# Order of the first loads, a row of identity products at the start, and the order of the last output blocks in a fused attention and two-MLP kernel

## The chip, the cores and the metric

The kernel runs on one core of one Trainium2 chip. The metric is the device time of one execution in microseconds (us); lower is better. The core has five engines that run side by side and meet through semaphores: TensorE (PE in the profile, with its weight loads as PEld), VectorE (DVE), ScalarE (ACT), GpSimd (POOL) and SyncE (SP), which here only issues DMAs. Each engine works through its own instructions in order, so an instruction that waits holds up everything behind it on that engine.

## The reference

Inputs are q, k and v of shape (4, 12, 448, 64), and the weights of two gated MLPs.

```python
scores = q @ k.T / sqrt(64) - log(448)
attn_out = sigmoid(scores) @ v                       # per batch and head
x = attn_out with the heads side by side             # (4, 448, 768)

# MLP 1, then MLP 2 with its own weights
h = act(x @ w_in)                                    # relu, then gelu (tanh form)
u, v = h[..., :512], h[..., 512:]
v_n = (v - mean(v)) / sqrt(var(v) + 1e-6)            # MLP 2 also times g_ln
v_s = einsum('ts,bsd->btd', w_spatial, v_n) + b_spatial[None, :, None]
x = (u * v_s) @ w_out                                # MLP 2 adds its input x
```

The weights w_in and w_out arrive as 8-byte floats, the others as 4-byte ones.

## The kernel before

Most products are made in a fast 4-byte matmul format whose operands are split into a high part (a rounded copy) and a low part (the rest), three products for one. Values times attention is made in plain 4-byte floats.

**Attention** runs over NG = 12 groups of four heads (three groups for each of four batches) in steps s = 4n + r, where n is the group and r a block of 128 keys (the last has 64). Step s issues, in this order: `scores(n, r)` on PE (L357) and the sigmoid of them on ACT (L368); `values` of step s - 2 on PE (L381), which adds up in two PSUM banks for a group; at r = 1 `gather(n - 1)` on DVE (L395), which copies the previous group's sums out of those two banks; and one third of the operands of group n + 1: `turn` (transposes, DVE, r = 0), `high` (copies, DVE and ACT, r = 1), `low` (subtractions, L337, one half on DVE and one on POOL, r = 2). The pool for the value sums has two banks in all, so the first `values` of group n + 1 (step 4n + 6) waits for `gather(n)` (step 4n + 5).

Loads are issued by SP in program order. Before the loop come `load_qk(0)`, `load_qk(1)` (two DMAs each) and `load_v(0)` (eight DMAs). In the loop `load_v(1)` comes at s = 0, `load_qk(n + 2)` at r = 1 and `load_v(n + 2)` at r = 2, so values are two groups ahead.

**Conversion of the weights** is spread over the run by a `Belt`: each `tick(new)` moves every running job by one stage and then starts `new` more. A job `convert` is: load 256 KB (SP, L158); make a 4-byte float from the 8-byte one (DVE L169, L173, L177, with a square on POOL L164 or ACT L168); finish it (DVE L183); cast the high part (ACT L191); subtract for the low part (L193). In attention one piece starts in each of the steps 0 to 7 and then in every second step. A second belt, `spatial`, does the same for the four slices of `w_spatial` with `load_w_sp`: four DMAs; nothing; transpose and two casts on DVE (L226 to L228); subtract and copy on DVE (L230, L231). A slice has one of two buffers. It ticks from s = 42 on, so slice j is transposed at step 44 + j.

**The MLPs** run block by block: for each batch `hv` (L474) makes the half that is normalised, `hu` (L519) the other, `sp` (L538) the product over the sequence, and `wo` (L572) the output product. After each of these comes a `fill`, which ticks the belts. `split_x` (L462 on ACT, L463 on DVE) makes the high and low part of a block's input; for the first block it stands at s = 48, behind the last scores.

**The end.** The last `wo` runs over six output columns blocks m; when one is done DVE adds the input (L582). `store_last` then transposes block c on PE (L609) with the identity, copies it out of PSUM (ACT L616, DVE L614) and stores it (L620, L623), in pairs of blocks. It is called for block m - 2 behind the products of block m.

Of the kernel before, what the change touches and what calls it, by code (L numbers as in the profile page):

```python
# [9 lines left out]
F32 = mybir.dt.float32  # L10
# [15 lines left out]
def tile_sigmoid_attention_two_gated_mlps(  # L26
# [59 lines left out]
    def bank():  # L86
        return later["ps_t"].tile([P, 512], F32, tag="t", name="t")
# [186 lines left out]
    def attention(apool, epool, ps_att, done):  # L274
# [13 lines left out]
        def load_v(n):  # L288


            b, i = divmod(n, G)
            vt = epool.tile([P, 4, 3, D], F32, tag="v", name="vt", bufs=3)
            vr = epool.tile([P, 2, D], F32, tag="vr", name="vr", bufs=3)
            src = v[b, 4 * i:4 * i + 4].rearrange("h (t c) d -> t h c d", c=TC)
            for e in range(4):
                ts = slice(32 * e, 32 * e + 32)
                nc.sync.dma_start(
                    out=vt[ts].rearrange("p h c d -> p h (c d)"),
                    in_=src[:, :, 3 * e:3 * e + 3].rearrange("t h c d -> t h (c d)"),
                )  # L300
                hs = slice(2 * (e // 2), 2 * (e // 2) + 2)
                nc.sync.dma_start(out=vr[ts], in_=src[:, hs, 12 + e % 2])
            vs[n] = vt, vr
# [106 lines left out]
        load_qk(0)  # L410
        load_qk(1)
        load_v(0)
        turn(0)
        high(0)
        low(0)
        for s in range(4 * NG + 2):
# [9 lines left out]
            if n + 1 < NG:  # L426
# [3 lines left out]
                    high(n + 1)  # L430
                elif r == 2:
                    low(n + 1)
            if n + 2 < NG:
                if r == 1:
                    load_qk(n + 2)
                elif r == 2:
                    load_v(n + 2)
            if s == 0:
                load_v(1)
            elif s == 4 * NG - 9:  # L440
                load_vecs(l1)
            belt.tick(1 if s < 8 else s % 2)
            if s >= 4 * NG - 6:
                spatial.tick(1)
        return lambda: gather(NG - 1)

# [1 line left out]
    class Mlp:  # L448
# [111 lines left out]
        def wo(self, b, i, after=None):  # L560
# [8 lines left out]
            for m in range(KD):  # L569
# [7 lines left out]
                for c in done if i == KF - 1 else ():  # L577
                    x = xs[b // 2][:, c, (b % 2) * S:(b % 2 + 1) * S]
                    if L.n == 1:
                        nc.scalar.copy(out=x, in_=self.o[c][:, :S])  # L580
                    else:
                        nc.vector.tensor_tensor(out=x, in0=self.o[c][:, :S], in1=x, op=ALU.add)  # L582
                if after and m > 1:
                    after(m - 2)
            if after:
                after(KD - 2)
                after(KD - 1)

    def store(pool, b, m):

# [13 lines left out]

    def store_last(o, pr, m):

        t = bank()
        for j in range(3, 7):
            nc.tensor.transpose(  # L609
# [2 lines left out]
        dst, src = o[:, :, m * P:(m + 1) * P], t.rearrange("p (j f) -> p j f", j=4)  # L612
        if m == KD - 2:
            nc.vector.tensor_copy(out=dst, in_=src)  # L614
        else:
            nc.scalar.copy(out=dst, in_=src)  # L616
        if m % 2:
            ms = slice((m - 1) * P, (m + 1) * P)
            eng = nc.scalar if m == KD - 1 else nc.sync
            nc.sync.dma_start(  # L620
                out=out[2 * pr + 1, :3 * P, ms].rearrange("(j p) m -> p j m", p=P), in_=o[:, 1:, ms]
            )
            eng.dma_start(out=out[2 * pr + 1, 3 * P:, ms], in_=o[REST:, 0, ms])  # L623

    with tc.manual_schedule():
        make_identity(nc, ident)
# [22 lines left out]
        with tc.tile_pool(name="fpool", bufs=1) as fpool:  # L649
# [9 lines left out]
            for n, (m, b) in enumerate(seq):  # L659
# [3 lines left out]
                def fill(new=0, more=(), waits=False):  # L663
# [8 lines left out]
                    if waits:  # L672
                        chain.tick()

                def split_next(c):
                    if nxt:
                        nxt.split_x(nb, c, c + 2)
# [39 lines left out]
                m.sp(b, 1)  # L717
                fill(0 + refill, waits=True)
                m.wo(b, 0)
                fill(1, w_o(0))  # L720
                split_next(2)
                m.sp(b, 2)
                if refill:
                    spatial.waiting = [load_w_sp(l2, j) for j in range(4)]
                fill(0 + refill, waits=True)
                m.wo(b, 1)
                fill(1, w_o(1))
                split_next(4)
                m.sp(b, 3)
                fill(1, waits=True)  # L730
                m.wo(b, 2)
                fill(0 + refill, w_o(2))
                if refill:
# [44 lines left out]
```

## Time and profile before

| | us |
|---|---|
| median of 3 runs | 597.12 (595.78 to 597.28) |
| the profiled execution, its own time | 597.48 |
| its span, first to last instruction | 595.7 |

| engine | busy us | share of the span |
|---|---|---|
| PE | 571.4 | 96% |
| DVE | 410.0 | 69% |
| ACT | 251.6 | 42% |
| POOL | 98.9 | 17% |

The page gives the busy time of each engine over the span, and what an engine waited for. Since PE is busy nearly all the time, one reads first where it is not: a table of the run in stretches shows that. In each stretch one then looks for the wait that ended last. All times in the rows are counted from the span's start.

### The profile page before, as it was taken

The page shows a single profiled execution, that of the slowest core. Times are in us where ns is not written, and L with a number is a line of the kernel's source. Part 1 is how long each engine was busy: PE and PEld are TensorE (multiplying, and loading weights), DVE is VectorE, ACT ScalarE, POOL GpSimd, SP SyncE. Part 2 cuts the span into 40 slices and gives each one's busy share as a digit, 9 for nine tenths or more (in the row PEclk, how much of TensorE's full clock was granted, in tenths as well). Part 3 has the DMA queues.
Part 4 walks back from the last instruction along what each step waited for, and adds up shares of the span by engine and source line. Part 5 has one row for each costly group of instructions (what it writes and reads, how often), then busy time and mean ns, then how long its engine had stood idle before and what let it go on. Part 6 is the DMA issues. An engine that isn't in the chain of part 4 may idle for free.

```text
span 595.7 us, 9520 instructions
## 1 busy us (share of the span) xinstructions
PE 571.4 (96%) x3568; PEld 456.5 (77%) x3568; DVE 410.0 (69%) x805; ACT 251.6 (42%) x418; POOL 98.9 (17%) x127
## 2 busy tenths in 40 slices
PE   4969999999999999999999999999999999999996
PEld 2535555555469888998888899888989988998995
DVE  4599999999976985894688357669444545544433
ACT  4647877787724434433423345534221313212112
POOL 0445465445221001000200100020010002001000
PEclk9979999999999999999999999999999999999999
DMA  6854446545311212532242224520004100500502
GB/s 185 226 182 136 139 145 196 166 138 119 62 60 35 72 53 72 159 107 62 87 153 80 80 73 114 123 54 18 1 1 77 17 0 12 83 1 0 82 13 92
DMA packets 85405, 51.74 MB, mean 87 GB/s; under 512 B 56112, under 2 KB 75376, under 8 KB 85360
## 3 DMA queue, kind: packets, MB, share of 16 engines
q1 hardware_dynamic: 85280, 51.08, 31.7%
q8 instruction: 28, 0.46, 0.3%
q14 instruction: 17, 0.14, 0.1%
q10 hardware_dynamic: 80, 0.07, 0.0%
HBM read 41.68 MB, written 9.44 MB: 86 GB/s over the span
## 4 chain that ended last, share of the span: by engine, by line
PE 73%; DVE 13%; DMA 4%; issue 3%; ACT 3%; POOL 2%; SPq 1%; DVEq 0%; ACTq 0%
PE t L519 13%; PE t L474 12%; PE sc L572 12%; PE av L381 10%; PE sc L357 10%; PE t L538 10%; PE av L572 6%; DMA w<-in_moe_w_in_dram 2%; DVE f L177 2%; DVE f L173 1%; DMA inq<-in_q_dram 1%; DVE st L483 1%; DVE f L183 1%; POOL st L488 1%; DVE vr L493 1%
## 5 line engine op out<-in xcount | busy, mean ns | idle before, releaser
L368 ACT ACTIVATE a<-sc,small 128x896 f32<-128x896 f32 (+1 forms) x96 | 92.8, 1006 | 32.6 <-PE sc L357 32.3
L357 PEld LDWEIGHTS sc<-ops 32*128 32x128 f32 x1152 | 57.5, 194 | 46.5 <-ACT a L368 25.2
L357 PE MATMUL sc<-ops 32*128 32x448 f32 x1152 | 80.0, 397 | 9.0 <-ACT ops L328 7.5
L519 PE MATMUL t<-xh,uh 128*128 128x448 f32 x192 | 69.9, 364 | 0.9 <-ACT u L523 0.9
L485 POOL TENSOR_SCALAR st<-st 128x1 f32<-128x1 f32 x28 | 10.6, 378 | 356.7 <-DVE st L484 356.7
L381 PE MATMUL av<-a,vt 128*64 128x448 f32 x288 | 64.7, 572 | 5.2 <-DVE x L395 5.0
L519 PE MATMUL t<-xh,ul 128*128 128x448 f32 x192 | 69.5, 362 | 0.0
L519 PE MATMUL t<-xl,uh 128*128 128x448 f32 x192 | 69.3, 361 | 0.0
L474 PE MATMUL t<-vh,xl 128*128 128x512 f32 x168 | 65.7, 391 | 1.3 <-DVE xl L463 1.2
L538 PE MATMUL t<-sh,v 128*128 128x448 f32 x224 | 65.9, 363 | 0.6 <-DVE gt L544 0.6
L474 PE MATMUL t<-vh,xh 128*128 128x512 f32 x168 | 65.6, 390 | 0.0
L474 PE MATMUL t<-vl,xh 128*128 128x512 f32 x168 | 65.4, 389 | 0.0
L551 ACT CAST gh<-u 128x448 fp32r<-128x448 f32 x32 | 18.2, 567 | 103.6 <-DVE u L550 103.6
L483 DVE BATCH_NORM_STATS2 st<-vr 128x6 f32<-128x512 f32 x28 | 19.4, 694 | 53.6 <-ACT vr L480 53.6
L183 DVE SCALAR_TENSOR_TENSOR f<-g,f 128x256 f32<-128x256 f32 x72 | 47.1, 654 | 9.2 <-ACT g L168 3.9
L572 PE MATMUL sc<-gl,oh 128*128 128x448 f32 x128 | 46.7, 365 | 2.1 <-DVE gl L555 2.1
L572 PE MATMUL sc<-gh,oh 128*128 128x448 f32 x128 | 46.5, 363 | 0.0
L572 PE MATMUL sc<-gh,ol 128*128 128x448 f32 x128 | 46.4, 362 | 0.0
L538 PE MATMUL t<-sl,v 128*128 128x448 f32 x128 | 46.3, 362 | 0.0
L538 PEld LDWEIGHTS t<-sh,v 128*128 128x128 f32 x224 | 42.0, 188 | 3.9 <-DVE gt L544 1.2
L381 PEld LDWEIGHTS av<-a,vt 128*64 128x64 f32 x288 | 18.2, 140 | 34.8 <-issue 25.6
L501 ACT CAST v<-vr 128x512 fp32r<-128x512 f32 x24 | 14.9, 621 | 66.0 <-DVE vr L493 66.0
(87 smaller groups left out, 1019.4 us busy)
## 6 DMA issues: line engine op xcount, KB each, us to landing
w<-in_moe_w_in_dram SPq DMA_DIRECT2D x48, 256.0 KB, 3.6
w<-in_moe_w_out_dram SPq DMA_DIRECT2D x24, 256.0 KB, 2.8
ink<-in_k_dram SPq DMA_DIRECT2D x12, 448.0 KB, 4.2
inq<-in_q_dram SPq DMA_DIRECT2D x12, 448.0 KB, 5.1
vt<-in_v_dram SPq DMA_DIRECT2D x48, 96.0 KB, 2.5
out_dram<-y SPq DMA_DIRECT2D x72, 56.0 KB, 1.9
kept<-f SPq DMA_DIRECT2D x30, 128.0 KB, 1.7
w<-kept SPq DMA_DIRECT2D x12, 192.0 KB, 2.6
```

Source lines behind the costliest of these rows:

```text
L177: nc.vector.scalar_tensor_tensor(out=f, in0=high, scalar=-0x40000000, in1=f, op0=ALU.bitwise_and, op1=ALU.bitwise_or)
L183: nc.vector.scalar_tensor_tensor(out=f, in0=g, scalar=TINY * TINY, in1=f, op0=ALU.is_ge, op1=ALU.mult)
L357: nc.tensor.matmul(sc[h // 2][:, h % 2, :S], w[ps, o:o + P], ops[n][ps, y, S * j:S * (j + 1)], start=(t == 0), stop=(t == 5), tile_positio ...
L368: nc.scalar.activation(a[:, 2 * x:2 * x + 2] if r < 3 else a[ps], sc[x][ps, :, :S], AF.Sigmoid, bias=bias_s[ps], scale=scale,)
L381: nc.tensor.matmul(avp[n][x][o * D:(o + 1) * D, :S], vt[:, h, r] if r < 3 else vr[ps, o], a[:, h] if r < 3 else a[ps, o], start=(r == 0), ...
L474: nc.tensor.matmul(ps[:, :FF], a, w[:, c, :], start=(c == 0 and n == 0), stop=(c == KD - 1 and n == 2),)
L483: nc.vector.bn_stats(out=st, in_=vr)
L501: nc.scalar.copy(out=pair[0], in_=vr)
L519: nc.tensor.matmul(ps[:, :S], w, a, start=(c == 0 and n == 0), stop=(c == KD - 1 and n == 2))
L538: nc.tensor.matmul(ps[:, :S], a, w, start=(n == 0), stop=(n == len(todo) - 1))
L551: nc.scalar.copy(out=gh, in_=u)
L572: nc.tensor.matmul(self.o[m][:, :S], w, a, start=(i == 0 and n == 0), stop=(i == KF - 1 and n == 2),)
```

## The change

In words:

- Values are loaded one group ahead instead of two: `load_v(n + 1)` at r = 2, in two buffers instead of three; `load_v(1)` goes from s = 0 to s = 2.
- The first piece of weights is started ahead of the loop, right behind `load_v(0)`; step 0 doesn't tick, so every later piece starts in the step in which it did.
- 18 products of the identity with itself stand ahead of everything else on PE; nothing reads them.
- `load_vecs` and the four `w_spatial` slices start two steps earlier (37 instead of 39, 40 instead of 42).
- In the first MLP block three of the fills start no new piece.
- At the end `store_last` is called three blocks late instead of two; the last block's add is split in two, its copy between ACT and DVE; blocks 4 and 5 are stored one by one; and the short DMA of a pair goes ahead of the long one.

```diff
-            vt = epool.tile([P, 4, 3, D], F32, tag="v", name="vt", bufs=3)
-            vr = epool.tile([P, 2, D], F32, tag="vr", name="vr", bufs=3)
+            vt = epool.tile([P, 4, 3, D], F32, tag="v", name="vt", bufs=2)
+            vr = epool.tile([P, 2, D], F32, tag="vr", name="vr", bufs=2)
...
         load_v(0)
+        belt.tick(1)
+
+        warm = ps_att.tile([P, 2, 512], F32, tag="sc", name="sc")
+        for _ in range(18):
+            nc.tensor.matmul(warm[:, 0, :P], ident, ident, start=True, stop=True)
         turn(0)
...
-            if n + 2 < NG:
-                if r == 1:
-                    load_qk(n + 2)
-                elif r == 2:
-                    load_v(n + 2)
-            if s == 0:
-                load_v(1)
-            elif s == 4 * NG - 9:
+            if r == 1 and n + 2 < NG:
+                load_qk(n + 2)
+            elif r == 2 and n + 1 < NG:
+                load_v(n + 1)
+            if s == 4 * NG - 11:
                 load_vecs(l1)
-            belt.tick(1 if s < 8 else s % 2)
-            if s >= 4 * NG - 6:
+            if s > 0:
+                belt.tick(1 if s < 7 else s % 2)
+            if s >= 4 * NG - 8:
                 spatial.tick(1)
...
-                    else:
-                        nc.vector.tensor_tensor(out=x, in0=self.o[c][:, :S], in1=x, op=ALU.add)
-                if after and m > 1:
-                    after(m - 2)
+                        continue
+                    h = S - 2 * P if after and c == KD - 1 else 0
+                    for ts in ((slice(0, h), slice(h, S)) if h else (slice(0, S),)):
+                        nc.vector.tensor_tensor(
+                            out=x[:, ts], in0=self.o[c][:, ts], in1=x[:, ts], op=ALU.add
+                        )
+                if after and m > 2:
+                    after(m - 3)
             if after:
-                after(KD - 2)
-                after(KD - 1)
+                for m in range(KD - 3, KD):
+                    after(m)
...
         if m == KD - 2:
             nc.vector.tensor_copy(out=dst, in_=src)
+        elif m < KD - 2:
+            nc.scalar.copy(out=dst, in_=src)
         else:
-            nc.scalar.copy(out=dst, in_=src)
-        if m % 2:
-            ms = slice((m - 1) * P, (m + 1) * P)
+            nc.scalar.copy(out=dst[:, :2], in_=src[:, :2])
+            nc.vector.tensor_copy(out=dst[:, 2:], in_=src[:, 2:])
+        if m % 2 or m == KD - 2:
+            ms = slice((m if m > 3 else m - 1) * P, (m + 1) * P)
             eng = nc.scalar if m == KD - 1 else nc.sync
+            eng.dma_start(out=out[2 * pr + 1, 3 * P:, ms], in_=o[REST:, 0, ms])
             nc.sync.dma_start(
                 out=out[2 * pr + 1, :3 * P, ms].rearrange("(j p) m -> p j m", p=P), in_=o[:, 1:, ms]
             )
-            eng.dma_start(out=out[2 * pr + 1, 3 * P:, ms], in_=o[REST:, 0, ms])
...
+                rate = 0 if n == 0 else 1
...
-                fill(1, w_o(0))
+                fill(rate, w_o(0))
...
-                fill(1, w_o(1))
+                fill(rate, w_o(1))
...
-                fill(1, waits=True)
+                fill(rate, waits=True)
```

## Rows read from the trace of the kernel before

**Rows 1.** Table of stretches: stretch, length, busy us of each engine, clock, DMA, GB/s

```profile
30.00:40.00 10.00, 4.99 (x31) 2.10 (x30) 9.86 (x16) 3.45 (x5) 5.41 (x6) 0.67 0.76 233
40.00:60.00 20.00, 20.00 (x218) 10.28 (x214) 18.80 (x32) 14.90 (x19) 9.28 (x10) 0.99 0.38 115
160.00:170.00 10.00, 8.73 (x49) 4.32 (x42) 9.79 (x22) 5.53 (x9) 1.50 (x2) 1.00 0.50 129
200.00:220.00 20.00, 18.46 (x89) 16.59 (x90) 18.07 (x42) 9.12 (x21) 0.00 (x0) 1.00 0.15 46
580.00:596.00 16.00, 10.49 (x61) 9.02 (x60) 6.09 (x10) 3.50 (x6) 0.00 (x0) 0.91 0.27 86
```

**Rows 2.** The same table, narrower, ahead of the first values of group 1

```profile
33.50:35.63 2.13, 0.00 (x0) 0.00 (x0) 2.13 (x3) 0.84 (x1) 1.83 (x2) 0.50 0.37 123
```

**Rows 3.** The chain of work that ended last, 0 to 41 us: start, length, what

```profile
2.12 7.70 DMA inq<-in_q_dram
...
15.40 7.80 DMA w<-in_moe_w_in_dram
...
23.58 3.60 DMA w<-in_moe_w_in_dram
...
32.57 2.18 DVE f L177
...
35.63 3.25 PE av L381 x8
```

**Rows 4.** Timeline, 0 to 36 us: start, length, engine, line, operation [idle <-releaser]

```profile
1.00 0.29 POOL masks.py:199 TENSOR_SCALAR_AFFINE_SELECT ident<-ident 128x128 f32<-128x128 f32 x1
...
7.55 3.36 PE L357 MATMUL sc<-ops 32*128 32x448 f32 x26 [7.55 <-ACT ops L328]
...
10.19 0.43 SPq L297 DMA_DIRECT2D vt<-in_v_dram  x1
...
13.96 0.43 SPq L158 DMA_DIRECT2D w<-in_moe_w_in_dram  x1
...
18.38 0.29 DVE L169 TENSOR_SCALAR f<-w 128x256 int32<-128x256 int32 x1 [6.25 <-DMA w<-in_moe_w_in_dram]
...
21.72 1.72 PE L381 MATMUL av<-a,vt 128*64 128x448 f32 x8
...
28.80 1.82 PE L357 MATMUL sc<-ops 32*128 32x448 f32 x24
...
32.31 2.16 POOL L337 TENSOR_TENSOR ops<-tq,ops 128x896 fp32r<-128x896 f32 x1
...
34.67 1.68 DVE L395 COPY x<-av 128x448 f32<-128x448 f32 x2
```

**Rows 5.** Timeline, 150 to 172 us, end of attention, same columns

```profile
152.65 0.42 DVE L177 SCALAR_TENSOR_TENSOR f<-w,f 128x256 int32<-128x256 int32 x1
...
155.55 1.94 DVE L395 COPY x<-av 128x378 f32<-128x378 f32 x8 [0.84 <-PE av L381]
...
157.16 1.72 PE L381 MATMUL av<-a,vt 128*64 128x448 f32 x8
...
163.55 0.62 DVE L230 TENSOR_TENSOR sl<-tsp,sh 128x448 fp32r<-128x448 f32 x1
...
164.31 0.50 PE L474 MATMUL t<-vh,xh 128*128 128x512 f32 x1
...
164.38 0.65 DVE L226 STREAM_TRANSPOSE tsp<-wsp 128x448 f32<-128x448 f32 x1
...
165.47 4.25 DVE L463 TENSOR_TENSOR xl<-x,xh 128x512 fp32r<-128x512 f32 x6
166.21 0.50 PE L474 MATMUL t<-vh,xl 128*128 128x512 f32 x1 [1.17 <-DVE xl L463]
```

**Rows 6.** Timeline of SP, the last stores, same columns

```profile
590.61 0.50 SPq L623 DMA_DIRECT2D out_dram<-ol  x1
591.50 0.37 SPq L620 DMA_DIRECT2D out_dram<-ol  x1
```

## The prediction

> **What bounds the kernel now.** I read the table of stretches first, for PE. From 40 us on PE is busy almost without a break [rows 1]; what it lacks there is 1.3 us at the end of attention (160 to 170) and 1.5 us in the first MLP block (200 to 220). The large gaps are at the two ends: 5.0 of the 10 us from 30 to 40, and 5.5 us from 580 on. So what the change can win lies in the first 40 us and the last 10.
>
> In the first 40 us I read the chain of waits [rows 3]. It is no chain of matmuls: a q load (2.12, 7.70 us), a weight piece (15.40, 7.80 us), another piece (23.58, 3.60 us), DVE's conversions, then the first values of group 1 at 35.63. The timeline shows the wait itself: PE ends the scores of step 6 at 28.80 + 1.82 = 30.62 and stands until 35.63 [rows 3, 4], because `gather(0)`, which frees the two banks, starts on DVE only at 34.67 [rows 4]. DVE is late because it works in order: its first conversion waited 6.25 us for the first piece [rows 4]. During PE's wait the granted clock falls to 0.50, half of full speed (1.2 of 2.4 GHz) [rows 2], and the values then take 3.25 us where warm ones take 1.72 [rows 3, 4].
>
> Why do the loads come late? SP issues about one DMA in 0.47 us, and the chain shows a second limit: the 12th DMA goes out when the 4th has landed (2.12 + 7.70 = 9.82), the 32nd when the 24th has (15.40 + 7.80 = 23.20) [rows 3]. Eight are in flight, no more.
>
> **The change part by part. Order of the first loads.** In the order before, the first piece is DMA 21, behind the eight of `load_v(1)`, which begin at 10.19; it goes out at 13.96 [rows 4]. Now it is DMA 13 and takes the place at 10.19: 3.77 us earlier, and so do k, q of group 2 and the second piece. The eight value DMAs follow, and the third piece is behind them, as it was. By the rule of eight in flight it goes out when the second piece has landed. Here I must choose. If that takes 7.80 us as before, the shift stays 3.8 us. The nearest like case is the start: four big loads (1.84 MB) with small value loads behind them were all landed 9.82 - 0.72 = 9.1 us after the first issue; here they are 1.44 MB, so between 7.1 us (all of it scales with the bytes) and 9.1 (none): I take the middle, 10.19 + 8.1 = 18.3 instead of 23.2. That gives 4.9 us; the end with 7.1 gives 5.9. From the third piece's landing to the first values of group 1 there lie 35.63 - 27.18 = 8.45 us of DVE work [rows 3]: the piece, `turn(2)`, the next piece, the first copy of `gather(0)`. None of it is changed. So these values start at 35.63 - 4.9 = 30.7 (29.6 to 31.8).
>
> PE must be ready by then. At the pace of before the scores of step 6 end at 30.62. With a warm clock from the start the first three steps would save some 4 us (an estimate: half of the 3.36 us of the first scores [rows 4] and of what follows them), so 26.5. Both lie ahead of 30.7, so PE's own speed before that point is covered by the loads.
>
> **18 identity products.** The identity is there at 1.29 [rows 4]. Four value products in two column pairs take 1.72 us warm [rows 4], so one of 128 columns is estimated at 0.86 x 128/448 = 0.25 us, 0.5 at half clock; 18 are 4.4 to 8.8 us and end between 5.7 and 10.1, against the first scores at 7.55 [rows 4]. An overrun can cost 2.5 us at the first scores, and a warm clock can win the 4 us estimated above. Both are hidden by the wait up to 30.7, so I put 0; if that cover were gone, the products would be worth between -4 and +2.5 us.
>
> **The clock in the wait.** PE's wait becomes up to 4.2 us (from 5.0). In the row the clock fell some 2.8 us into the wait. It may fall again or not; a stay saves 3.25 - 1.72 = 1.5 us in the values and about 0.7 in the scores behind them.
>
> **Values one group ahead.** A `load_v` is issued four steps (some 12 us) ahead of its use and lands within 6 to 7 us. Its wait, for the values of the group two back, is the same event as before, since there is one buffer less and one group less lead. Behind it on SP stand only later pieces. 0.
>
> **Spatial slices two steps earlier.** A transpose with its casts takes 165.47 - 164.38 = 1.1 us of DVE, a subtraction 0.8 [rows 5]. Before, only slice 0's transpose lay ahead of `gather(10)` (step 45) on DVE. Now there are also its subtraction, all of slice 1 and the transpose of slice 2: 0.8 + 1.9 + 1.1 = 3.8 us. And SP has now the DMAs of slice 2 (which wait for slice 0's transpose to free the buffer) ahead of the weight piece of step 43, so that piece goes out near 154 and lands near 157, and DVE waits for it 1 to 2 us ahead of the gather. DVE had 0.84 us to spare at 155.55 and PE 0.6 at 157.16 [rows 5]: the gather comes some 4.7 us late and PE stands some 4 us at the first values of group 11. In return the backlog which made DVE start the low parts of x at 165.47, and PE wait 1.17 and 0.5 us for them [rows 1, 5], is gone. Carried through: values of group 11 from 161.2 instead of 157.16, 4.0 later, and from there 7.15 us of PE to the first `hv` (157.16 to 164.31 [rows 5]), in which the matmuls' wait of 1.17 [rows 5] and one of 0.5 behind it fall away, with some 0.3 of refilling: 4.0 - 2.0. Cost 2.0 us; none if DVE has slack that I don't see, 4.2 if the clock falls in that wait too.
>
> **Three pieces fewer in block 0.** The waits from 200 to 212 [rows 1] come from the nine pieces started earlier; the three that are left out are converted from 213 on, where PE never waits. They shift the belt by three, to the last fills of block 2 and the first of block 3, which have room. 0, give or take 0.5.
>
> **The end.** PE no longer waits for the first add, and the last copy is halved: the last block is out of PSUM about 0.3 us earlier. But SP has now two more stores (0.4 to 0.5 us of issue each) ahead of the last one [rows 6], which goes out at about 591.95 instead of 591.50, with half the bytes. Half of its 384 KB at the pace of the first loads (1.84 MB in 9.1 us, latency included) is 0.95 us less to move; I take 0.85. Net 0.45 - 0.85 = -0.4, between +0.5 (the bytes cost nothing) and -1.0 (SP isn't late).
>
> **Sum.** -4.9 (loads) + 2.0 (spatial) - 0.4 (end) = -3.3, and the clock at even odds in both waits adds 0.5 x (2.2 - 2.2) = 0; rounded with the small chance of free slack, -3.5. The profiled execution took 597.48 (span 595.7 and 1.8 around it), so 594.0 there; its time is 0.36 above the median of the runs, 597.12, and against that the forecast is **593.6**.
>
> **The rivals.** *Both gains are larger:* the clock stays up in the first wait (2.2), and DVE's 2.18 us for L177, which stood still while POOL's L337 ran 2.16 us [rows 3, 4], meets POOL at another moment and takes its 0.42 [rows 5], 1.75 less: -4.9 - 2.2 - 1.75 + 2.0 - 0.4 = -7.3, 589.8. Against it: both engines are released by the same `turn(2)`, so their order should repeat. The Trainium skill, SBUF — State Buffer, section Who interferes with whom, says that the port pair shared by VectorE and GpSimd is an exclusive lock and that issue order decides who blocks; by that rule this rival needs only a small shift of order. *Given back:* the clock falls in both waits: -4.9 + 4.2 - 0.4 = -1.1, 596.0. For it: the new wait at 157 is as long as the remaining one at 26. *Slower:* the piece behind slice 2's DMAs lands as slowly as the slowest weight load of the trace, 7.80 us [rows 3] instead of the some 3 assumed. DVE then reaches `gather(10)` 5 us later still, PE stands 9 us and the clock falls: -4.9 + 2.0 + 5 + 2.2 - 0.4 = +3.9, 601.0. It turns slower once that piece takes over 6 us or so. Against it: nothing but four small slices shares the queue then. *The change doesn't do what it says:* the first piece goes out earlier but lands no earlier than the backlog allows; then the shift is less than 3.8 and the time is that of the second rival.
>
> **How the numbers follow.** Forecast 0.47, larger gain 0.23, given back 0.22, slower 0.08. Faster by over 0.3% (1.8 us, about what a measurement of this kernel can tell from no change) means under 595.3: the first two, 0.70; within it 0.22; slower 0.08. The range takes in the larger gain and the given-back case: 589.0 to 597.2.
>
> **What would show it.** After: first DMA of a piece at about 10.2; DVE's first L169 near 13.5; first values of group 1 near 30.7 (a start near 27 would mean that PE, not the loads, set it; one at 34 or later that the loads didn't move). Identity products from 1.3, ended by 10. A PE wait of some 4 us near 153 (157 less the gain) on L395, and none on L463 behind it: if that wait isn't there, the spatial step is wrong. The last SP store about 0.4 us later against the last copy.

## The result and the profile after

The changed kernel takes 599.99 us (median of 18 runs, 598.36 to 602.37) against 596.92 for the kernel before beside it: a ratio of 1.0052, interval 1.0041 to 1.0064, so some 3 us slower. The forecast was 593.6 with a range up to 597.2; the time lies above it. The profiled execution has a span of 598.7 us, 3.0 more than that of before.

The table of stretches of the changed kernel, with the columns of [rows 1]:

```profile
30.00:40.00 10.00, 10.00 (x122) 5.74 (x120) 9.69 (x17) 6.93 (x9) 4.95 (x7) 1.00 0.60 190
40.00:60.00 20.00, 17.72 (x170) 8.83 (x166) 17.37 (x26) 13.21 (x17) 10.44 (x9) 0.91 0.40 118
150.00:160.00 10.00, 4.09 (x32) 1.91 (x30) 7.50 (x20) 3.19 (x4) 2.93 (x4) 0.79 0.53 150
160.00:170.00 10.00, 10.00 (x63) 5.57 (x62) 7.14 (x15) 5.54 (x9) 0.75 (x1) 0.87 0.11 28
```

PE's gap from 30 to 40 us is gone (4.99 busy in [rows 1], 10.00 here). In its place there is a gap of 2.3 us in the stretch 40 to 60, which was full before, and one of 5.9 us from 150 to 160. The timeline of the changed kernel tells what stands behind each. First the start (start, length, engine, line, operation, idle time and releaser):

```profile
1.35 6.32 PE L417 MATMUL sc<-ident 128*128 128x128 f32 x36 [1.35 <-POOL ident masks.py:199]
...
9.84 0.43 SPq L158 DMA_DIRECT2D w<-in_moe_w_in_dram  x1
...
13.51 0.29 DVE L169 TENSOR_SCALAR f<-w 128x256 int32<-128x256 int32 x1 [1.07 <-DMA w<-in_moe_w_in_dram]
...
17.36 1.99 SPq L158 DMA_DIRECT2D w<-in_moe_w_in_dram  x3
...
21.66 0.29 DVE L169 TENSOR_SCALAR f<-w 128x256 int32<-128x256 int32 x1 [1.32 <-DMA w<-in_moe_w_in_dram]
...
27.04 0.42 DVE L177 SCALAR_TENSOR_TENSOR f<-w,f 128x256 int32<-128x256 int32 x1
27.21 2.20 POOL L337 TENSOR_TENSOR ops<-tq,ops 128x896 fp32r<-128x896 f32 x1 [0.49 <-ACT ops L328]
27.38 1.71 DVE L395 COPY x<-av 128x448 f32<-128x448 f32 x2
28.35 1.76 PE L381 MATMUL av<-a,vt 128*64 128x448 f32 x8 [1.41 <-DVE x L395]
...
31.48 1.72 PE L381 MATMUL av<-a,vt 128*64 128x448 f32 x8
...
42.64 2.75 PE L381 MATMUL av<-a,vt 128*64 128x448 f32 x8 [2.28 <-DVE x L395]
...
47.33 1.72 PE L381 MATMUL av<-a,vt 128*64 128x448 f32 x8
```

The last three rows of the same work in the kernel before (its first values of group 2, at 49.70, have no wait):

```profile
40.90 1.73 PE L381 MATMUL av<-a,vt 128*64 128x448 f32 x8
...
49.70 1.73 PE L381 MATMUL av<-a,vt 128*64 128x448 f32 x8
...
52.79 1.72 PE L381 MATMUL av<-a,vt 128*64 128x448 f32 x8
```

The 18 products stand there as 36 rows, two for each. The first values of group 1 start at 28.35 instead of 35.63 [rows 3], 7.3 us earlier, and the second at 31.48 instead of 40.90, 9.4 earlier, since the granted clock doesn't fall at this wait as it did before. But at the first values of group 2 PE waits 2.28 us for `gather(1)`, a wait that the profile of before doesn't have; the granted clock is 0.50 from 44 to 46 us, the values take 2.75 us, and behind them (47.33 instead of 52.79) 5.5 us are left. The scores of step 46 start at 149.71 in place of 155.44, so 5.7 us are carried through attention.

The end of attention, same view, 145 to 168 us:

```profile
146.30 1.88 SPq L215 DMA_DIRECT2D wsp<-in_moe_w_spatial_dram  x4
...
148.27 0.42 SPq L158 DMA_DIRECT2D w<-in_moe_w_out_dram  x1
...
149.71 1.81 PE L357 MATMUL sc<-ops 32*128 32x448 f32 x24
...
152.33 0.29 DVE L169 TENSOR_SCALAR f<-w 128x256 int32<-128x256 int32 x1 [3.26 <-DMA w<-in_moe_w_out_dram]
152.66 0.72 DVE L173 SCALAR_TENSOR_TENSOR f<-w,f 128x256 uint32<-128x256 uint32 x1
153.41 0.83 DVE L177 SCALAR_TENSOR_TENSOR f<-w,f 128x256 int32<-128x256 int32 x1
...
156.33 1.90 DVE L395 COPY x<-av 128x378 f32<-128x378 f32 x8
...
157.44 3.25 PE L381 MATMUL av<-a,vt 128*64 128x448 f32 x8 [5.91 <-issue]
...
160.62 2.41 PE L357 MATMUL sc<-ops 32*128 32x448 f32 x24
...
165.83 4.26 DVE L466 TENSOR_TENSOR xl<-x,xh 128x512 fp32r<-128x512 f32 x6 [2.72 <-ACT xh L465]
...
167.03 0.50 PE L477 MATMUL t<-vh,xh 128*128 128x512 f32 x1
```

Here the gain is lost. PE stands 5.91 us ahead of the first values of group 11. The row says "issue", which means that the profile shows no releaser; the program's order gives it: these values write the banks that `gather(10)` empties, and its copies start at 156.33, 1.1 us ahead of them. The gather is late because DVE stood 3.26 us for a weight piece (issued at 148.27 behind four DMAs of slice 2) and then had that piece and the slices to work off. In the table of stretches PE is at 0.79 clock there, and from 156 to 162 us the granted clock is 0.50; values take 3.25 instead of 1.72 us and the scores 2.41 instead of 1.5. The first `hv` comes 17.32 us behind the start of step 46's scores (167.03 - 149.71). Before it was 164.31 - 155.44 = 8.87, with 1.17 and 0.5 us of waiting for `xl` behind it, which is now gone. So 8.45 - 1.7 = some 6.7 us are lost, and the 5.7 won have become 1.0 lost. From the first `sp` to the last the changed kernel takes 1.8 us longer than the kernel before (386.20 against 384.43 between their starts), and the rest of the run 0.3. 1.0 + 1.8 + 0.3 = 3.1.

### The profile page after: what moved, and what is told of

Same layout as the page of the kernel before. It is cut to its first block, busy times and chain, and to the rows that moved or that the text cites. A ratio compares the mean times of both kernels' runs of the same rounds, so it can differ in the third digit from the quotient of the medians.

```text
span 598.7 us, 9595 instructions
## 1 busy us (share of the span) xinstructions
PE 575.6 (96%) x3604; PEld 461.5 (77%) x3604; DVE 409.8 (68%) x807; ACT 251.9 (42%) x418; POOL 99.8 (17%) x127
## 4 chain that ended last, share of the span: by engine, by line
PE 67%; DVE 15%; DMA 6%; issue 5%; ACT 3%; POOL 2%; SPq 1%; DVEq 0%; ACTq 0%
PE t L477 12%; PE sc L575 11%; PE av L381 10%; PE t L522 10%; PE sc L357 10%; PE t L541 9%; PE av L575 6%; DMA w<-in_moe_w_in_dram 4%; DVE f L173 2%; DVE f L177 2%; DVE f L183 2%; DVE st L486 1%; DVE f L169 1%; POOL st L491 1%; DMA vt<-in_v_dram 1%
## 5 line engine op out<-in xcount | busy, mean ns | idle before, releaser
L357 PEld LDWEIGHTS sc<-ops 32*128 32x128 f32 x1152 | 56.2, 187 | 39.3 <-ACT a L368 24.4
L357 PE MATMUL sc<-ops 32*128 32x448 f32 x1152 | 77.4, 387 | 2.4 <-ACT a L368 1.8
L183 DVE SCALAR_TENSOR_TENSOR f<-g,f 128x256 f32<-128x256 f32 x72 | 48.7, 677 | 10.8 <-ACT g L168 5.3
```

Source lines behind the costliest of these rows:

```text
L183: nc.vector.scalar_tensor_tensor(out=f, in0=g, scalar=TINY * TINY, in1=f, op0=ALU.is_ge, op1=ALU.mult)
L357: nc.tensor.matmul(sc[h // 2][:, h % 2, :S], w[ps, o:o + P], ops[n][ps, y, S * j:S * (j + 1)], start=(t == 0), stop=(t == 5), tile_positio ...
```

## The experiments

The runs e1 to e14 were timed in five rounds beside the kernel before, with 6 to 12 executions each; ratios are to that kernel. "Spatial early" stands for `load_vecs` at step 37 and slices from 40, "spatial as before" for 39 and 42.

| run | median us | ratio (95% interval) |
|---|---|---|
| changed kernel | 599.99 | 1.0052 (1.0041 to 1.0064) |
| changed, spatial as before (e1) | 594.71 | 0.9950 (0.9929 to 0.9970) |
| before, spatial early alone (e2) | 602.92 | 1.0085 (1.0060 to 1.0110) |
| before, load order alone (e3) | 597.54 | 0.9997 (0.9981 to 1.0013) |
| before, identity products alone (e4) | 598.20 | 1.0012 (0.9990 to 1.0034) |
| before, end alone (e5) | 597.05 | 1.0005 (0.9991 to 1.0019) |
| before, rate alone (e6) | 597.22 | 0.9993 (0.9978 to 1.0008) |
| changed, places as before (e7) | 598.79 | 1.0033 (1.0019 to 1.0047) |
| changed, four slice buffers (e8) | 595.89 | 0.9975 (0.9959 to 0.9991) |
| before, load order and identity (e9) | 593.56 | 0.9941 (0.9921 to 0.9961) |
| changed, stand filled (e10) | 601.32 | 1.0067 (1.0050 to 1.0085) |
| changed, spatial late (e11) | 593.13 | 0.9946 (0.9926 to 0.9967) |
| e11 with end and rate of before (e12) | 593.11 | 0.9937 (0.9913 to 0.9961) |
| e8 with the stand filled (e13) | 594.42 | 0.9946 (0.9927 to 0.9965) |
| e13 with places as before (e14) | 593.23 | 0.9933 (0.9907 to 0.9960) |

### Is it the spatial slices?

My theory after the traces: the two steps by which the slices are earlier cost 6 us, and all else together wins 3. The rival: the new start itself runs into the end of attention, whatever the slices do. e1 takes the slices' part out of the changed kernel, e2 puts it alone into the kernel before.

```diff
-            if s == 4 * NG - 11:
+            if s == 4 * NG - 9:
                 load_vecs(l1)
...
-            if s >= 4 * NG - 8:
+            if s >= 4 * NG - 6:
                 spatial.tick(1)
```

> The changed kernel with load_vecs and the w_spatial slices back at the steps of before (39 and 42); all else as changed. Theory S (the stall of 5.9 us at the first values of group 11 comes from the slices: their DVE work, and a weight piece that SP can send only behind slice 2's loads, stand ahead of gather(10)): the stall goes, the clock stays up there, DVE again makes the low parts of x late by 1 to 2 us; the end of the first hv comes about 5 to 6.6 us earlier, time about 593.5 to 595, ratio to before 0.994 to 0.997. Rival V (the stall comes from values loaded one group ahead, whose eight loads now stand at step 42): stall and clock fall stay, time 599 to 600.

> The kernel before with load_vecs and the slices two steps earlier, alone. Theory S: a stall of 4 to 6 us at the first values of group 11, a fall of the clock behind it, some 1.7 us of it given back at the first hv: time 601 to 603.5, ratio 1.007 to 1.011. Rival V: no stall of over 1 us, time within 0.3% of before.

e1 is 0.0102 of the time, 6.1 us, faster than the changed kernel; e2 is 5.1 us slower than the kernel before. Its PE stands 4.76 us at the first values of group 11. In the timeline of e1 that stand is not there:

```profile
150.31 1.79 PE L357 MATMUL sc<-ops 32*128 32x448 f32 x24
152.02 1.72 PE L381 MATMUL av<-a,vt 128*64 128x448 f32 x8
...
161.37 0.50 PE L477 MATMUL t<-vh,xl 128*128 128x512 f32 x1 [1.46 <-DVE xl L466]
```

Step 46's scores start as early as in the changed kernel, the values follow without a break, and the old wait for `xl` is back. The slices are the cause, with either start.

### What does the new start win, and which half of it?

e3 has the load order and the two buffers, e4 the identity products, e9 both (with the three value buffers of before).

```diff
         load_v(0)
+        belt.tick(1)
+        warm = ps_att.tile([P, 2, 512], F32, tag="sc", name="sc")
+        for _ in range(18):
+            nc.tensor.matmul(warm[:, 0, :P], ident, ident, start=True, stop=True)
         turn(0)
```

(e3 without the three lines of `warm`, e4 without the tick; the other lines of the load order, as in the change, are left out here.)

> The kernel before with the order of loads alone: values one group ahead in two buffers, the first piece ahead of the loop; no identity products. If the loads alone set the start (as in the prediction): first values of group 1 near 28.5, the same steady state, time 591 to 592.5, ratio 0.990 to 0.993. If the identity products had a part in it (rival): the first scores stay cold to about 19 us, the wait ahead of group 1 is shorter, and the gain is 1 to 3 us less: 593 to 595. If values one group ahead are the harm (rival V): a stall near 155, 596 or more.

> The kernel before with the 18 identity products alone. Prediction's theory (PE's pace ahead of the first values of group 1 is hidden by the loads): the products end near 7.7, scores 0 to 3 at full speed, but the first values of group 1 stay at 35.6 and the time within 0.3% of before. Rival: the warm clock alone is worth 2 us or more, 595 or less.

> The kernel before with the two changes of the start alone: the load order (with the three buffers of before) and the 18 identity products; spatial slices, rate and end as before. The version of the changed kernel with only the slices put back gave 594.7 us. If the rate and the end are worth nothing together, this gives 594.7 within 0.5; if they cost what the trace of the changed kernel shows (about 0.3 us at the end, up to 1.0 us in the second and third block), it gives 593.5 to 594.4.

Alone each is worth nothing that can be measured; together they win 0.59%, 3.5 us. The timeline of e3 shows why the loads alone don't:

```profile
28.45 1.81 PE L357 MATMUL sc<-ops 32*128 32x448 f32 x24
30.19 1.72 PE L381 MATMUL av<-a,vt 128*64 128x448 f32 x8
...
45.40 2.19 PE L381 MATMUL av<-a,vt 128*64 128x448 f32 x8 [2.57 <-DVE x L395]
...
164.89 0.50 PE L473 MATMUL t<-vh,xl 128*128 128x512 f32 x1 [2.70 <-DVE xl L462]
```

The values of group 1 follow the scores without a wait: PE itself is the later one, and starts at 30.19. Its scores take 2.61 us up to 17.4 and 1.49 only from 19.95 on; with the products (e9) they take 1.49 from 10.92 on. PE is then done with the scores of step 6 at 26.7 in e9 and 26.9 in the changed kernel, 3.3 to 3.5 us sooner than in e3, waits for DVE, and starts the values 2 us sooner (28.20 and 28.35). What e3 does win (step 46's scores at 152.23, where the five profiles with the loads of before have 152.37 to 155.44) it gives back at the first `hv`, which waits 2.70 us for `xl`. In e4 the reverse: PE's scores take 1.50 us from 10.95 on, then it stands 6.78 us for `gather(0)`, which the loads hold back, and the values run in 3.25 us. The two halves need each other. The products don't hold the clock up in every execution: in the profiles of e1 and e10 the granted clock is 0.50 again from 13.7 to 17.1 and from 11.2 to 18.0 us, and PE is the later one there, at 28.24 and 29.26.

### What is the stand of 5.91 us made of?

Three parts can be told apart: the late weight piece, DVE's work on the slices ahead of `gather(10)`, and the clock that falls while PE stands. e8 gives the slices four buffers, so SP needn't wait for slice 0's transpose and the piece goes out early.

```diff
-        w = stg.tile([P, S], F32, tag="sp", name="wsp", bufs=2)
+        w = stg.tile([P, S], F32, tag="sp", name="wsp", bufs=4)
```

> The changed kernel with four w_spatial slice buffers in place of two, so that SP can issue all four slices in a row and the weight piece w_out of the second set behind them without waiting for slice 0's transposes. It asks what the 5.91 us stand of PE ahead of the first values of group 11 is made of. If the late piece does it (in the changed kernel DVE's first operation on it waits 3.26 us for the DMA and the gather of group 10 that PE waits for stands right behind it), the wait of DVE shrinks to under 1 us, PE's stand to under 3.5 us, the clock may stay up (2.4 us more), and the time falls by 3 to 5 us, to 595 to 597. If the DVE and ACT work that the slices bring ahead of the gather does it, PE's stand stays at 5 to 6 us and the time within 1 us of the changed kernel's 600.0.

0.77% faster than the changed kernel, 4.6 us. The timeline of e8:

```profile
149.76 1.81 PE L357 MATMUL sc<-ops 32*128 32x448 f32 x24
149.87 0.28 DVE L169 TENSOR_SCALAR f<-w 128x256 int32<-128x256 int32 x1
150.19 0.43 DVE L173 SCALAR_TENSOR_TENSOR f<-w,f 128x256 uint32<-128x256 uint32 x1
150.65 0.42 DVE L177 SCALAR_TENSOR_TENSOR f<-w,f 128x256 int32<-128x256 int32 x1
...
152.91 1.90 DVE L395 COPY x<-av 128x378 f32<-128x378 f32 x8
...
154.02 3.25 PE L381 MATMUL av<-a,vt 128*64 128x448 f32 x8 [2.46 <-issue]
...
163.87 0.50 PE L477 MATMUL t<-vh,xh 128*128 128x512 f32 x1
```

DVE no longer waits for the piece, the gather starts at 152.91 instead of 156.33, and PE's stand shrinks from 5.91 to 2.46 us. That rest is DVE's work: it runs without a break up to the gather. The clock falls all the same (values 3.25 us). To take that out, products with the identity fill the stand: 18 in the changed kernel (e10), 9 in e8 (e13).

```diff
             if s > 1:
+                if s == 4 * NG - 2:
+                    warm2 = ps_att.tile([P, 2, 512], F32, tag="sc", name="sc")
+                    for _ in range(18):
+                        nc.tensor.matmul(warm2[:, 0, :P], ident, ident, start=True, stop=True)
                 values(*divmod(s - 2, 4))
```

> The changed kernel with 18 extra identity products on PE behind the scores of step 46, where PE stands 5.91 us for the gather of group 10; it computes nothing new, the products' sums are read by nobody. It asks what the fall of the clock after that stand costs by itself. If the fall is worth what the rows say (values 3.25 in place of 1.72 us and scores 2.41 in place of about 1.5 us behind the stand: some 2.4 us), the first hv of the second set starts about 2.4 us earlier than the 167.03 us of the changed kernel and the time falls by 2 to 2.5 us, to about 597.6. If PE at full clock then only waits for the next step's DVE or ACT work, under 0.7 us comes of it.

> The changed kernel with four slice buffers and, behind the scores of step 46, 9 identity products that nobody reads. With the four buffers alone PE stands 2.46 us there and then runs values in 3.25 and scores in 2.61 us. If the clock stays up, that work takes 1.7 to 1.9 and 1.5 us, the first hv starts 2 to 2.5 us nearer to step 46's scores (14.1 us behind them with the four buffers alone, 11.6 to 12.1 here), and if nothing else is late next the time falls from 595.9 to 593.5 to 594. If the first hv then waits for xl (2.90 us of DVE's wait for ACT's xh stand there) or the gain is lost later, as in the first try, the time stays within 0.7 us of 595.9.

The timeline of e13, where the clock stays at 1.00 from 152 to 160 us:

```profile
149.99 1.79 PE L357 MATMUL sc<-ops 32*128 32x448 f32 x24
151.71 2.27 PE L431 MATMUL sc<-ident 128*128 128x128 f32 x18
154.19 1.91 PE L381 MATMUL av<-a,vt 128*64 128x448 f32 x8 [0.21 <-issue]
156.04 1.50 PE L357 MATMUL sc<-ops 32*128 32x448 f32 x24
...
161.53 0.50 PE L481 MATMUL t<-vh,xh 128*128 128x512 f32 x1
```

The first `hv` is 11.54 us behind step 46's scores instead of e8's 14.11, and the ratio falls from 0.9975 to 0.9946, 1.7 us (the two intervals overlap by 0.0006). So with the piece on time the clock's share shows: 2.6 us in the trace, some 1.7 in the time. In e10 the same edit brings `hv` nearer by 1.9 us (17.32 to 15.41), and this is still there at the first `sp`; but the time does not fall, the ratio is 1.0067 against 1.0052, intervals overlapping. In its profile two losses stand against the 1.9 us. One lies ahead of the edit and can't come from it: step 46's scores start at 151.35, 1.6 us behind the changed kernel's, after the fall of the clock from 11.2 us on. The other comes later: from the first `sp` to the last 388.33 us against 386.20, with longer waits for `gt` (the sum of an `sp` that DVE takes out of PSUM) in blocks of the second MLP, one of them where DVE waited 3.34 us for the store of an output block, after 1.47 us for the one ahead of it. What links this to the products I haven't found; e13 has the same edit with half as many and not that loss.

From step 46's scores to the first `hv` the traces therefore split the 8.45 us, in the order in which the parts were taken out: late piece 3.2 (17.32 to 14.11), clock 2.6 (14.11 to 11.54), and what is left, DVE's work on the slices, 2.7 (11.54 to 8.87). In the time the piece was worth 4.6 us, with an uncertainty of some 1.2 by the two intervals; the traces place only 3.2 of them.

### Where do the blocks lose 1.8 us?

One part can be seen in the groups of instructions by shape: products of `sp` with the high part of `w_spatial`, 224 of them, in the kernel before, in the changed one and in e7 (count, busy us, mean ns of one, idle time before them).

```profile
L538 PE MATMUL t<-sh,v 128*128 128x448 f32 x224 | 65.9, 363 | 0.6 <-DVE gt L544 0.6
```

```profile
L541 PE MATMUL t<-sh,v 128*128 128x448 f32 x224 | 66.6, 367 | 1.8 <-DVE gt L549 0.9 <-DVE gt L547 0.9
```

```profile
L542 PE MATMUL t<-sh,v 128*128 128x448 f32 x224 | 65.9, 363 | 2.0 <-DVE gt L550 1.1 <-DVE gt L548 0.9
```

The changed kernel's products take 367 ns, those of before 363. e2 has 367 too, e1 363 to 364: it goes with the early slices. Over all sixteen profiles the mean is 366.6 to 367.9 ns in the five with early slices and nothing done about places (the changed kernel, e2, e8, e10, e13), and 362.8 to 363.9 in the other eleven, e7 and e14 among them. Since the slices are now made ahead of the first piece of `w_out`, `sh` and `sl` get their places in SBUF ahead of the first tiles of `o`. e7 changes nothing but that order of placing, by one line ahead of the allocation of `sh`:

```diff
         if L.sh is None:
+            L.part_o(0, slice(0, PIECE))
             L.sh = wts.tile([P, 4, SPAN], F32R, tag="sh", name=f"sh{L.n}")
```

> The changed kernel with the halves of o for the first block put in SBUF ahead of the halves of w_spatial, the order that the kernel before has; no instruction is added, taken away or moved in time. It asks where the slow drift of some 1 us between the first block and the last comes from: sp products take 2.23 us a set in the changed kernel and in the one with only the spatial slices early, 2.20 us in the kernel before. If the places do it, sp sets go back to 2.20 us, and the time falls by 0.6 to 1.2 us, to about 599. If the drift has another cause (other work of the slices' new time), sp stays at 2.23 us and the time at 600.0 within 0.4.

The products are back at 363 ns, first `sp` to last takes 385.30 instead of 386.20 us, and the ratio falls by 0.0019, 1.1 us, with intervals that overlap. The length of the products is the firm part: 3.4 ns on the 224 and 3.2 on the 128 that read `sl` are some 1.2 us. So the places cost about 1 us. Why the one place is slower the runs don't show. The other 0.9 us of the blocks are scattered waits of PE for DVE's `gt` and `gl` (the low part of the gated product); I didn't trace them to a part of the change. They may be scatter: five profiles with the slices and the blocks of before (the kernel before, e3, e4, e5, e9) take 384.23 to 385.41 us from the first `sp` to the last, and e1, with 363 ns, takes 386.90. The fills are not it:

```diff
+                rate = 0 if n == 0 else 1
...
-                fill(1, w_o(0))
+                fill(rate, w_o(0))
```

(and the same in the two other fills)

> The kernel before with only the rate of three fills of the first block changed from 1 to 0. The prediction had this at 0 within 0.5 us. In the changed kernel the second and the third block each end about 0.5 us later against the kernel before. If those 1.0 us come from the three pieces that are carried over to a later fill, this kernel is 0.5 to 1.2 us slower than the kernel before; if they come from the spatial slices or the places in SBUF, it lies within 0.4 us of the kernel before.

First `sp` to last is 384.44 us in e6 against 384.43 before, and the time is the same. For the end, e5 has the three hunks of the change that concern `wo`, its `after` and `store_last`:

```diff
-                if after and m > 1:
-                    after(m - 2)
+                if after and m > 2:
+                    after(m - 3)
```

> The kernel before with only the changes of the end: the last turned two blocks on, the last add and the last copy split, three stores in place of two. The prediction had this at -0.4 us (-1.0 to +0.5). In the changed kernel the last block is ready as long after the last wo as before, but its store on SP goes out some 0.7 us later behind the stores of the two blocks ahead of it, and only a small part of that comes back in a shorter landing: by that this kernel is 0 to 0.6 us slower than the kernel before. If the prediction's sum was right and the changed kernel's end is only shifted by its start, it is 0.4 us faster.

1.0005, 0.9991 to 1.0019: nothing that can be measured. The trace is finer: from the start of the last `sp` to the end of the span it is 17.82 to 17.91 us in the seven profiles with the old end, and 18.13 to 18.19 in the nine with the new one. So the new end costs 0.3 us. The last stores of the changed kernel show where:

```profile
593.71 0.42 DVE L627 COPY ol<-t 128x256 f32<-128x256 f32 x1 [0.20 <-ACT ol L626]
593.79 0.48 SPq L631 DMA_DIRECT2D out_dram<-ol  x1
594.31 1.18 SPq L632 DMA_DIRECT2D out_dram<-ol  x2
```

The last block is ready at 594.13, but its store is the second of the two in the last row and goes out at 595.00, since three others stand ahead of it on SP. In [rows 6] the last store went out at 591.50, 0.03 us behind its copy. With half the bytes it lands 2.66 us later instead of 3.07.

### Do the causes add up, and is there a faster order?

e14 puts the three remedies into the changed kernel (four buffers, 9 products, places); e11 moves the slices the other way, to begin at step 46, behind the last gathers; e12 is e11 with the end and the rate of before.

```diff
-            if s >= 4 * NG - 8:
+            if s >= 4 * NG - 2:
                 spatial.tick(1)
```

> As the run before it, and the halves of o for the first block placed ahead of the halves of w_spatial as in the kernel before. It asks whether the causes add up. Late piece -4.1, places -1.2, clock -2 to -2.4 us from the changed kernel's 600.0 give 592.3 to 592.7, and sp sets back at 2.20 us (363 ns a product). If the clock's part doesn't come out in the time, it gives 594.5 to 595.

> The changed kernel with the spatial slices later than in either kernel: the second set's vectors at step 39 as before, and the slices from step 46 on in place of 40 (changed) and 42 (before). If what decides is that DVE, ACT and the queue are free for the last gathers and for xl of the first block, the stand ahead of the first values of group 11 and the wait of the first hv for xl (1.46 us with the slices as before) both go and it lands at 593 to 594.5, at or under the 594.7 us with the slices as before. If the slices then come too late for the first sp, which needs all four, PE waits there for the transposes or their splits, and the time is 597 or more.

> As the kernel with the late spatial slices, but with the end and the rate of the kernel before. It asks whether the end and the rate are worth anything where the start is not disturbed. By the trace of the changed kernel they cost 0.3 to 1 us, so this should lie 0.3 to 1 us under the one with the late slices and be the fastest of all; by the prediction (-0.4 for the end, 0 for the rate) it lies 0.4 us above it.

e14 comes out at 0.9933, 593.2 us. By ratios the remedies are worth 4.6 + 1.7 + 0.8 = 7.1 us from the changed kernel's 600.0; the forecast from them was 592.3 to 592.7. They add up within the intervals, and DVE's 2.7 us, which the products only cover, are still in it. e11 gets to the same place with less: no stand and no wait for `xl`.

```profile
149.02 1.79 PE L357 MATMUL sc<-ops 32*128 32x448 f32 x24
150.73 1.72 PE L381 MATMUL av<-a,vt 128*64 128x448 f32 x8
...
157.89 0.50 PE L477 MATMUL t<-vh,xh 128*128 128x512 f32 x1
```

`hv` is 8.87 us behind the scores, without a wait behind it. Its 593.1 us and those of e12, e9 and e14 can't be told from each other; all four beat both kernels, by some 3.5 us the one and 6.5 the other. That e11 doesn't beat e9 by the 1.7 us of `xl` has a likely reason in the trace, which I didn't test: its `sp` and `hu` wait for `gt` and `u` 1.08, 0.76 and 0.56 us, as DVE has the slices to make then. The wait moves along with DVE's work. Between e12 and e11 no difference can be measured; the 0.3 us of the end are too few for that.

## Why the prediction was wrong

**What bounds the kernel** was read rightly: the two ends and the end of attention. But the rows of one execution made the first gap look larger than it is on the whole. The starts of step 46's scores in the five profiles with the old load order (the kernel before, e2, e4, e5, e6) run from 152.37 to 155.44, and the kernel before's own is the latest of them; in the ten with load order and products together (the changed kernel, e1 and e7 to e14) they lie between 149.02 and 151.35. Means of 154.0 and 149.9 give 4.1 us, and the time gives 3.5. My 4.9 is over both.

**The loads** went out as forecast: first piece at 9.84 (10.2), first L169 at 13.51 (13.5), third piece at 17.36 (18.3). The first values of group 1 came at 28.35, below my bounds of 29.6 to 31.8, and the term that was off is the DVE work behind the third piece's landing: I kept its 8.45 us, and it was 28.35 - 21.66 = 6.7. The difference is L177, 0.42 us in place of 2.18 [rows 3], what the first rival named; the third piece was there another 0.6 us early, inside my bounds. Here DVE's L177 starts at 27.04 and POOL's L337 at 27.21; before, POOL's was first, at 32.31, and L177 at 32.57 took 2.18 [rows 3, 4]. The Trainium skill, SBUF — State Buffer, section Who interferes with whom, says that the ports which VectorE and GpSimd share are an exclusive lock and that issue order decides who blocks; the rows agree: L177 takes 2.18 to 2.29 us in the six profiles in which L337 starts first, and 0.42 to 0.43 in the ten in which L177 does, and in e6 a lead of 0.06 us was enough for L337. I held the order to be fixed because both are released by one `turn`; it wasn't. Between `turn` and L337 stands ACT's cast L328:

```profile
31.29 0.94 ACT L328 CAST ops<-tq 128x896 fp32r<-128x896 f32 x1 [1.32 <-DVE tq L317]
```

```profile
26.20 0.94 ACT L328 CAST ops<-tq 128x896 fp32r<-128x896 f32 x1
```

Before, ACT stood idle and cast 0.03 us behind the end of `turn`; in the changed kernel it was still in a sigmoid and cast 0.48 us behind it, and that let L177 in first. In all sixteen profiles a cast up to 0.24 us late goes with L337 first, one from 0.38 us on with L177 first. The lead from this did not last: in e12 and e13, with the same start, L337 was first and the values of group 1 came at 31.00 and 30.20, near my 30.7; but they had no wait at group 2, and step 46's scores started at 150.71 and 149.99, within 0.9 us of the mean of 149.9. A smaller slip: the eight loads of a group took 6.9 to 8.1 us in the changed kernel, not my 6 to 7; four steps ahead of their use that cost nothing.

**What is late next** was missed there. I had looked at the stretch 40 to 60 in [rows 1], found it full, and let the gain pass through it. It was full because PE came late. The next wait on the same pair of banks, `gather(1)` ahead of the first values of group 2, took back 3.9 of the 9.4 us that had been won up to it: 2.3 by the wait and the rest by the clock behind it (31.48 is 9.4 early, 47.33 is 5.5).

**The identity products** lasted from 1.35 to 7.67, inside my 5.7 to 10.1. Alone they are worth nothing, as I said, hidden by the loads. In the changed kernel they aren't hidden: the loads came earlier than my 30.7, e3 shows PE without them as the later one at 30.19, and they carry most of the 3.5 us (0.9997 without them, 0.9941 with them).

**The spatial step is the one that failed**: +2.0 against 5 to 6 us. Its mechanism stands, link by link: the piece out late behind slice 2 (148.27, where my 154 less the 5.7 us is 148.3), DVE waiting for it, the gather late, PE standing, the wait for `xl` gone. Four sizes were off. The piece took 4.06 us from its issue to DVE's first operation on it (148.27 to 152.33), not 3; nor did only four small slices share the queue with it, as I had held: three DMAs of slice 2 were still under way and four of slice 3 went out before it landed. DVE's work from there to the gather took 4.00 us where e8 needs 3.04 for the same instructions (149.87 to 152.91): the landing released POOL in the same moment (its L164 starts at 152.37 and runs 0.73 us, L193 at 153.06 for 0.90), and L173 and L177 take 0.72 and 0.83 instead of 0.43 and 0.42. These two make the stand 5.9 instead of 4.0. Then the clock did fall; I had this as the bound of 4.2 but put it at even odds against a gain in the first wait that cancelled it. And the 1 us from the places in SBUF had no term at all: I looked at when the slices are made, and not at what else is decided by the order in which they are made. The rival "slower" named the right place, with another price: I let it decide by a landing of over 6 us, where 4.06, DVE's stretched work, the clock and the places together were enough.

**The end** came out 0.3 us longer instead of 0.4 shorter. The last store went out 0.87 us behind its copy where I had reckoned with 0.45, and half the bytes saved 0.4 us of its landing (2.66 for 3.07), not 0.85.

**The sum.** Start -3.5 for -4.9, spatial +5 to +6 for +2.0, end 0 to +0.3 for -0.4, rate 0 for 0: +1.5 to +2.8, against a measured +3.1 (2.4 to 3.8 by the interval). The direction was decided by one term whose bounds, 0 to 4.2, were too narrow on the side that mattered.

**The signs that I had listed** did their work: the wait near 157 less the gain with none for `xl` behind it was there, so the step was right in kind, and its length said at once that the size was wrong.

## What to carry to other kernels

A gain at the start has to pass every later wait on the same resource; look for the next one not in the stretches where PE has gaps now, but at the same pair of producer and consumer one turn further on. Work that is moved earlier on an in-order engine is paid three times: by its own length, by what waits for the DMAs that it is queued with, and by the clock if TensorE stands meanwhile; four buffers instead of two gave back 4.6 us here, and starting it behind the last urgent copy instead of ahead all of it. Two engines that are released by one event need not start in the same order each time, if a third stands between. And when a tile is made earlier, look at where it is now placed: here a pair of operands that moved changed all the products that read it.

## What the runs showed of the hardware that I had not expected

- The place of the operands `sh` and `sl` in SBUF changes the products that read them from 363 to 367 ns, and back when only the order of placing is changed (e7, e14): about 1 us in a run.
- A stand of PE of 2.46 us in e8 was as dear in what follows as one of 5.91 us in the changed kernel: values 3.25 us in both, scores 2.61 and 2.41. Filled with products the same steps take 1.91 and 1.50 us, the granted clock staying at 1.00.
- Executions of one kernel differ in the first 50 us: with the code of before the first values of group 1 start at 35.63 in one profile and at 32.63 in another (e2), and the wait at the first values of group 2 is there only in the second. In fifteen of the sixteen profiles the granted clock is down to 0.50 at or behind one of these two waits, in none at both.
